# Graph propagation with hop attention: the first bucket pass carries buckets and 16-bit patterns through its products, in one stated repeated order

## The chip, the cores and the metric

The kernel runs on one core of one Trainium2 chip. The metric is the device time of one execution in microseconds (us); of several runs the median is taken, and lower is better.

## The reference, cut to what matters

A graph has N = 10000 nodes with D = 128 features, and E = 160000 edges with random sources and targets (so 16 per node). Seven times every node receives the sum of its sources' features, scaled by both degrees; then each node attends over its eight tokens, and a readout weighs the tokens into one row.

```python
h, toks = x, [x]
for _ in range(K):                       # K = 7
    msg = h[src] * deg_inv_sqrt[src, None] * deg_inv_sqrt[dst, None]
    h = _segment_sum(msg, dst, N)
    toks.append(h)
tok = jnp.stack(toks, axis=1)            # (N, 8, 128)
t = _layernorm(tok)                      # then q, k, v, softmax over the 8 tokens, wo
o = tok + ...
alpha = _softmax(_layernorm(o) @ w_r)    # readout
return jnp.einsum('nk,nkd->nd', alpha, o)
```

The edges come as two lists of 64-bit integers in no order. Most of the kernel's first tenth turns them into a form that TensorE can multiply with.

## The kernel before, in words

The kernel has four stages: the **first bucket pass** (`pass_a` and `decode`), which sorts edges by blocks of 128 target nodes; the **second bucket pass** (`place`, `matrices`), which sorts by buckets of sources and builds 0/1 matrices, together with hop 1 (`hop1`), in an order written out by hand (the table FRONT); hops 2 to 7 (`block`); and the attention (the table ORDER). The change touches the first stage and what lies directly around it.

*First bucket pass.* A partition holds 1250 edges, in 25 chunks of 50 (NCH, B). The target's block (target >> 7, one of NK = 79) is an edge's key. Ahead of the loop, integer steps on VectorE (L307 to L313) make the key and two digits of a code of 24 bits, `d1` and `d2`, source >> 3 and the rest with the target's place in its block. `lag` (L254) compares the key columns of all chunks at distance 1 to 49 on VectorE (`eq`, L264) and adds the matches up in PSUM on TensorE (L266), which numbers an edge among equal ones in its chunk and partition. `first_rows` (L187) loads the node features and scales 79 groups of 128 rows on ScalarE (L198).

Each chunk then goes through this chain. `oh` (L226, VectorE) is the one-hot of 50 keys against 79 blocks, 3950 columns. `U` (L329, TensorE, 50 matmuls with a triangular matrix) counts equal keys in the partitions above; ScalarE copies it (L337). `ux` (L239, VectorE, 3950 columns) picks each edge's own count, and `R` (L243, L244, TensorE) folds it and adds the lag's number; `rk` (L247, VectorE) is the edge's rank in its block, that is, the partition in which it is to land. One-hots of the rank are made on VectorE for the first 18 of 50 edges (`rv`, L373) and on ScalarE for 32 (`rs`, L360, one ACTIVATE for each; `rb`, L341, gives their bias). The two products `o` (L232, VectorE, six steps of 1264 or 1422 columns) multiply `oh` by the digits, and `ta` (L385, TensorE, 50 matmuls of 158 columns) moves both digits into place by the ranks. `take` (L333, VectorE) adds the two halves into `TT`.

At the third chunk, `first_table` (L200) finds the largest magnitude of the scaled features by one reduction on VectorE (L205, 10112 columns), and writes the table of hop 1 as a high and a low float16 half: the high half on ScalarE (L177), the low one on VectorE (L178), four parts each, with stores to DRAM behind them (`rows`, L180).

*Decoding.* After the last chunk, `decode` (L389) turns all of `TT` (2000 columns) into the source's bucket `kB` and a 16-bit word, by eight integer and mixed steps on VectorE (L400 to L411), and `lag_rows` (L270) compares `kB` of all chunks at distance 1 to 24 (`eq`, L281), adds them up on TensorE (L285) and copies the result to `wB` (L288). The second pass needs `kB`, `word` and `wB`; its first instruction on VectorE is the one-hot of `kB` (L226 again, 3800 columns).

*What sets the order.* In the first pass a scheduler lays the instructions out; the loop's body in the code takes one chunk's products between the next chunk's counts and ranks, and engines run their own rows in the order laid out. Pools decide how far a chunk may run ahead: `oh`, `rs`, `rk` and PSUM tiles have two buffers, `rv`, `ux` and `o` one. GpSimd has nothing to do during the loop.

Of the kernel before, what the change touches and what calls it, by code (L numbers as in the profile page):

```python
# [58 lines left out]
2S1.2 0X1 3V1 1w0.2 2g2 3d1 3K3  # L59
"""  # L60


class Hops:
# [123 lines left out]
    def first_rows(self):  # L187
        nc, A = self.nc, self.nc.scalar
        tab0 = self.tab[0]
        y = self.tab[1].bitcast(F32)  # L190
        nc.gpsimd.memset(y[:, NT - 1:, :], 0.0)
        nc.gpsimd.memset(tab0[:, NT:, :], 0.0)
        h = NT // 2
        for a, b in ((0, h), (h, NT - 1)):
            nc.scalar.dma_start(y[:, a:b, :], self.x[a * 128:b * 128, :].rearrange("(t p) d -> p t d", p=128))
        nc.scalar.dma_start(y[:N - (NT - 1) * 128, NT - 1, :], self.x[(NT - 1) * 128:, :])
        for t in range(NT):
            A.activation(y[:, t, :], y[:, t, :], AF.Copy, scale=self.disT[:, t:t + 1])  # L198

    def first_table(self):  # L200
        nc, V = self.nc, self.nc.vector
        tab0, y = self.tab[0], self.tab[1].bitcast(F32)
        with self.tc.tile_pool(name="ft", bufs=1) as sp, self.tc.tile_pool(name="ftp", bufs=1, space=PSUM) as pp:
            mc = sp.tile([128, 1], F32, name="mc")
            V.tensor_reduce(mc, y[:, :NT, :], axis=mybir.AxisListType.XY, op=ALU.max, apply_absolute_value=True)  # L205
            q = self.pow2(pp, sp, mc, 2.0 ** 40)
            V.tensor_copy(self.sinv, q[:, 1:2])
            for a in range(0, NT, 20):
                b = min(NT, a + 20)
                self.to_table(y[:, a:b, :], tab0, q[:, 0:1], a, b)  # L210
                self.rows(0, tab0, a, b, nc.sync)
            V.tensor_scalar(self.ctok[0], self.disT, self.sinv, None, op0=ALU.mult)


            m2 = sp.tile([128, 1], F32, name="m2")
            V.tensor_reduce(m2, self.dis2, axis=X, op=ALU.max)
            V.tensor_scalar(m2, m2, 64.0 * BIG, None, op0=ALU.mult)
            q = self.pow2(pp, sp, m2, 2.0 ** 8)
            V.tensor_mul(self.sinv, self.sinv, q[:, 1:2])
            V.tensor_copy(self.q2, q[:, 0:1])  # L220


    def onehot(self, pool, name, key, n, size=None, **kw):
# [3 lines left out]
                                     self.io2[:, None, :n, :].to_broadcast([128, m, n, 2]), op=ALU.is_equal)  # L227
# [5 lines left out]

    def rank(self, wp, wu, R, oh, U2, w):

        nc, T = self.nc, self.nc.tensor
        m, nk, k = oh.shape[1], oh.shape[2], 5
        ux = wu.tile([128, m, nk, 2], F16, name="ux", tag="ux")
        nc.vector.tensor_tensor(ux, oh, U2[:, None].to_broadcast([128, m, nk, 2]), op=ALU.mult)  # L239
        R = R[:, :m * k * 2].rearrange("p (j k i) -> p j k i", k=k, i=2)  # L240
        for s in range(0, nk, k):
            e = min(k, nk - s)
            T.matmul(R[:, :, :e, :], self.id16, ux[:, :, s:s + e, :], start=s == 0, stop=False, skip_group_check=True)  # L243
        T.matmul(R[:, :, 0, :], self.id16, w, start=False, stop=True, skip_group_check=True)  # L244
        rk = wp.tile([128, m, 2], F16, name="rk")
        with nc.allow_low_precision("whole numbers; those over 2048 only have to stay large"):
            nc.vector.tensor_reduce(rk, R.rearrange("p j k i -> p j i k"), axis=X, op=ALU.add)  # L247
        return rk
# [21 lines left out]
    def lag_rows(self, ep, pp, key, w, m):  # L270

        V, T, k = self.nc.vector, self.nc.tensor, key.shape[2]
        n = 512 // k * k
        W = pp.tile([128, -(-m * k // n), 512], F32, name="W")
        flat = lambda z: z.rearrange("p m k -> p (m k)")
        parts = [(b, b * n, min(m * k, b * n + n)) for b in range(W.shape[1])]
        for b, r, e in parts:
            T.matmul(W[:, b, :e - r], self.id16, self.zero16[:, :e - r], start=True, stop=False, skip_group_check=True)
        for l in range(1, m):
            eq = ep.tile(list(key.shape), F16, name="eq")  # L280
            V.tensor_tensor(eq[:, l:], key[:, l:], key[:, :m - l], op=ALU.is_equal)  # L281
            for b, r, e in parts:
                r1 = max(r, l * k)
                if r1 < e:
                    T.matmul(W[:, b, r1 - r:e - r], self.id16, flat(eq)[:, r1:e], start=False, stop=(l + 1) * k >= e,  # L285
                             skip_group_check=True)
        for b, r, e in parts:
            self.nc.scalar.copy(flat(w)[:, r:e], W[:, b, :e - r])  # L288

    def pass_a(self):  # L290
        tc, nc, V, A, T, G = self.tc, self.nc, self.nc.vector, self.nc.scalar, self.nc.tensor, self.nc.gpsimd
        with ExitStack() as c:
# [5 lines left out]
            with tc.tile_pool(name="pe", bufs=1) as ep, tc.tile_pool(name="peq", bufs=3) as eqp, \  # L298
# [5 lines left out]
                it = ep.tile([128, 3, NCOL], I32, name="it")  # L304
                V.tensor_single_scalar(it[:, 0], ed[:, 1, :, 0], 7, op=ALU.arith_shift_right)
                A.copy(key, it[:, 0])
                V.tensor_single_scalar(it[:, 1], ed[:, 0, :, 0], 3, op=ALU.arith_shift_right)  # L307
                V.tensor_scalar(it[:, 2], ed[:, 0, :, 0], 7, 7, op0=ALU.bitwise_and, op1=ALU.logical_shift_left)
                V.tensor_single_scalar(it[:, 0], ed[:, 1, :, 0], 127, op=ALU.bitwise_and)
                V.tensor_tensor(it[:, 2], it[:, 2], it[:, 0], op=ALU.bitwise_or)  # L310
# [12 lines left out]

            def count(ch):
                oh = self.onehot(wp, "oh", K4[:, ch], NK)
                U = pp.tile([128, NK], F32, name="U")
                for j in range(NP):
                    for i in range(2):
                        T.matmul(U, self.tri, oh[:, j, :, i], start=j + i == 0, stop=j + i == NP)  # L329
                return oh, U  # L330

            def take(ch, ta):
                V.tensor_reduce(self.TT[:, ch, :NK], ta.rearrange("p h k -> p k h"), axis=X, op=ALU.add)  # L333

            def ranks(ch, oh, U):
                U2 = wp.tile([128, NK, 2], F16, name="U2")
                A.activation(U2, U[:, :, None].to_broadcast([128, NK, 2]), AF.Copy)  # L337
                rk = self.rank(wp, w1, pp.tile([128, 512], F32, name="R"), oh, U2, W4[:, ch])
# [1189 lines left out]
```

## Time and profile before

| | us |
|---|---|
| median of 3 runs | 3777.88 (3774.79 to 3786.38) |
| the profiled execution | 3821.03 |
| span of its trace | 3819.1 |
| second pass's first one-hot in the trace | 378.27 |

Mean granted clock of TensorE in the span: 0.976. Busy over the span: PE (TensorE) 94%, VectorE (DVE) 79%, ScalarE (ACT) 72%, GpSimd (POOL) 44%. The span is cut into 40 slices on the page, so that a slice is 95 us and the first pass fills the first four. Its digits there are tenths of busy time: PE 5 8 8 7, DVE 8 9 9 8, ACT 6 8 8 6, POOL 0 0 0 0.

How to read the rows: in a timeline, a row has the start and the duration in us, the engine, the line of the kernel, the operation, output<-inputs, their shapes, the count of merged instructions, and in brackets the idle time before them and what ended it. In a group, the busy time and the mean in ns stand behind the first bar, idle time before them behind the second. In the view of waits: engine and line, what it waited for, us in total, times, the longest.

### The profile page before, as it was taken

How to read it: one execution, taken by the hardware profiler on the slowest of the kernel's cores; microseconds unless marked ns; L12 is line 12 of the kernel's file. 1: busy time of each engine (PE TensorE's matmuls, PEld its weight loads, DVE VectorE, ACT ScalarE, POOL GpSimd, SP SyncE). 2: the span in 40 equal slices, each digit the busy share in tenths (PEclk: the TensorE clock that was granted, in tenths of full speed). 3: DMA queues.
4: the chain of work that ended last, by engine and by line, in shares of the span. 5: the costliest groups of instructions: out<-in, count | busy, mean ns of one | idle time of the engine just before them, and what ended most of it. 6: DMA issues, size and time to landing. Idle time of an engine off the chain costs nothing.

```text
span 3819.1 us, 173439 instructions
## 1 busy us (share of the span) xinstructions
PE 3594.5 (94%) x73707; PEld 2938.2 (77%) x73707; DVE 3019.8 (79%) x6994; ACT 2767.2 (72%) x6989; POOL 1681.5 (44%) x2230
## 2 busy tenths in 40 slices
PE   5887799999899999999999999999999998999997
PEld 4665678878688888887888788788878886777775
DVE  8998888888677777777777777777766665888888
ACT  6886488888766666766676666666756668888885
POOL 0000244444356656665666566566656661121111
PEclk8998899999999999999999999999999999999998
DMA  3100356556666666666666666666666552222220
GB/s 94 49 1 1 110 184 200 193 186 194 196 198 200 201 189 205 202 198 189 201 203 202 190 201 198 191 203 201 203 186 201 187 186 78 80 77 79 82 84 15
DMA packets 332728, 595.53 MB, mean 156 GB/s; under 512 B 57448, under 2 KB 225606, under 8 KB 326694
## 3 DMA queue, kind: packets, MB, share of 16 engines
q1 hardware_dynamic: 293989, 506.70, 42.5%
q0 software_dynamic: 35392, 72.55, 6.6%
q8 instruction: 577, 9.45, 1.0%
q10 hardware_dynamic: 2560, 5.12, 0.5%
q14 instruction: 210, 1.71, 0.2%
HBM read 455.49 MB, written 128.67 MB: 153 GB/s over the span
## 4 chain that ended last, share of the span: by engine, by line
PE 78%; DVE 9%; ACT 5%; DMA 4%; issue 3%; SPq 0%; POOL 0%; POOLq 0%; ACTq 0%; DVEq 0%
PE p L801 25%; PE acc L776 24%; PE acc L761 4%; PE pv L1172 4%; PE pu L1156 3%; PE p L667 3%; ACT rs L360 2%; PE po L1191 2%; PE pt L1146 2%; DVE o L232 2%; PE acc L654 2%; ACT eb L675 2%; PE acc L655 1%; PE ur L487 1%; PE ps L1221 1%
## 5 line engine op out<-in xcount | busy, mean ns | idle before, releaser
L806 ACT ACTIVATE eb<-p 128x512 f16<-128x512 f32 x2370 | 1258.3, 602 | 510.1 <-PE p L801 290.6
L808 DVE TENSOR_TENSOR eb<-p,eight 128x512 f16<-128x512 f32 x1896 | 1220.8, 686 | 328.3 <-PE acc L776 201.8
L801 PE MATMUL p<-tab,w 128*32 128x256 f16 x34128 | 1038.3, 274 | 20.1 <-issue 13.9
L776 PE MATMUL acc<-eb,w 128*128 128x256 f16 x8532 | 1011.7, 273 | 1.2 <-issue 1.2
L801 PEld LDWEIGHTS <-w 128*32 128x32 fp8e4 x34128 | 871.6, 97 | 161.9 <-issue 142.7
L776 PEld LDWEIGHTS <-w 128*128 128x128 fp8e4 x8532 | 835.5, 98 | 99.6 <-issue 2.0
L738 POOL DMA_INDIRECT og<-tabd,oidx x541 | 561.7, 1038 | 580.4 <-PE acc L776 286.6
L738 POOL DMA_INDIRECT og<-tabh,oidx x553 | 609.5, 1102 | 361.0 <-POOL og L737 121.9
L675 ACT ACTIVATE eb<-p 128x512 f16<-128x512 f32 x695 | 378.0, 626 | 30.6 <-PE p L667 24.8
L846 POOL TENSOR_SCALAR r<-s,ctok 128x128 f32<-128x128 f32 x474 | 293.5, 619 | 43.8 <-DVE s L792 26.4
L837 ACT ACTIVATE tab<-s,c 128x128 f16<-128x128 f32 x395 | 158.5, 401 | 200.9 <-DVE eb L808 172.3
L838 DVE SCALAR_TENSOR_TENSOR tab<-s,c,tab 128x128 f16<-128x128 f32 x395 | 138.9, 352 | 180.5 <-issue 169.3
L1261 POOL TENSOR_TENSOR p<-e,in 128x1024 f32<-128x1024 f32 (+1 forms) x40 | 76.5, 1913 | 446.5 <-DVE e L1260 446.5
L1213 ACT ACTIVATE junk<-tab 128x128 f32<-128x128 f32 x626 | 248.5, 401 | 8.3 <-SPq L1497 6.7
L667 PE MATMUL p<-tab,w 128*32 128x256 f16 x5688 | 210.7, 277 | 23.3 <-issue 12.4
L360 ACT ACTIVATE rs<-iof,rb 128x128 fp8e4<-128x128 f32 x784 | 231.8, 388 | 0.3
L792 DVE TENSOR_REDUCE s<-acc 128x128 f32<-128x256 f32 x474 | 196.9, 415 | 19.4 <-PE acc L790 11.7
L654 PE MATMUL acc<-eb,w 128*128 128x129 f16 x1422 | 203.4, 223 | 1.2 <-issue 0.4
L655 PE MATMUL acc<-eb,w 128*128 128x128 f16 x1422 | 201.5, 221 | 0.1
L737 POOL COPY og<-eb 128x1 f16<-128x1 f16 x452 | 83.1, 184 | 243.5 <-ACT eb L806 243.5
L667 PEld LDWEIGHTS <-w 128*32 128x32 fp8e4 x5688 | 137.8, 97 | 63.9 <-issue 41.4
L1172 PEld LDWEIGHTS pv<-Wv,xT 128*64 128x64 f32 x2504 | 138.9, 137 | 41.2 <-ACT uT L1157 29.3
(314 smaller groups left out, 5257.6 us busy)
## 6 DMA issues: line engine op xcount, KB each, us to landing
w<-gsd SPq DMA_DIRECT2D x474, 592.0 KB
gsd<-w SPq DMA_DIRECT2D x79, 592.0 KB
tok<-r SPq DMA_DIRECT2D x546, 64.0 KB
tab<-tok SPq DMA_DIRECT2D x273, 128.0 KB
rb<-srow SPq DMA_DIRECT2D x79, 352.0 KB
tabd<-tab SPq DMA_DIRECT2D x396, 64.0 KB
ra<-srow SPq DMA_DIRECT2D x79, 224.0 KB
og<-tabh,oidx POOLq DMA_INDIRECT x553
```

Of the source, the lines that this page charges most:

```text
L360: A.activation(ro[:, j - a, i, :], self.iof, AF.Abs_reciprocal_sqrt, scale=2.0 ** 21, bias=rb[:, j - VP, i:i + 1], saturate=False)
L654: T.matmul(acc[:, :129], W, rows[:, 128:257], start=start, stop=False, skip_group_check=True)
L667: T.matmul(p[32 * w:32 * w + 32, j], q["w", g][:, NJ * 128 + s * CAP:NJ * 128 + (s + 1) * CAP], tab[:, s, :], start=True, stop=True)
L675: A.activation(e[:, :, 0:256], pv, AF.Copy, scale=8.0)
L738: self.nc.gpsimd.indirect_dma_start(out=o, out_offset=None, in_=src[0] if i == NI else src[1], in_offset=bass.IndirectOffsetOnAxis(ap=self ...
L776: T.matmul(acc[0][:, :256], w[:, J * 128:(J + 1) * 128], e[:, j, :256], start=False, stop=J == NG - 1 and not late)
L801: T.matmul(p[32 * q:32 * q + 32, j], w[:, NJ * 128 + s * CAP:NJ * 128 + (s + 1) * CAP], tab[:, s, :], start=True, stop=True)
L806: A.activation(e[:, :n, 0:256], pv, AF.Copy, scale=8.0)
L808: V.tensor_tensor(e[:, :n, 0:256], pv, self.eight[:, :, None].to_broadcast([128, n, 256]), op=ALU.mult)
L846: self.nc.gpsimd.tensor_scalar(r, s, ct[:, t:t + 1], None, op0=ALU.mult)
L1172: T.matmul(p[64 * h:64 * h + 64, u - us[0], :], S[i]["xT"][:, h * m + q, 64 * c:64 * c + 64], Wv, start=True, stop=True, tile_position=(0, ...
L1213: A.activation(j, S[i]["x"][:, g, :], AF.Square, bias=S[i]["x"][:, g, 0:1], scale=-1.0, accum_out=R[i % 6][:, 0, g:g + 1])
```

## The change

What the products carry is changed. Before, two digits; now the bucket itself (`d1` from source >> 7 and a few integer steps) and a 16-bit pattern, an integer whose bits are read as a float16 (`d2` from `w16`). So the integer steps ahead of the loop grow from five to eleven on VectorE, and after `ta` nothing is left to decode: `kw` copies both halves from PSUM into one tile KW = [kB | word] on ScalarE, `take` and `decode` go. `low` restores the part of the code that TT has to hold, by one step on ScalarE and four of 80 columns on GpSimd, per chunk. Equal buckets are counted by chunk: `eq` compares all earlier chunks with this one (chunk number × 80 columns on VectorE), `W` adds them up on TensorE (as many matmuls of 80 columns), `wB` copies on ScalarE. `eqB`, `ux` and the last two products have one buffer; `rv` and the first product now two.

`first_table` becomes a generator. Its reduction is eight reductions of ten groups; the table is written in eight parts, the high half on ScalarE, the low half by a multiplication in place and a subtraction on GpSimd (L249, L250; 1280 columns each) instead of one step on VectorE. Of the 79 scalings of feature rows, 56 stay ahead of the loop, and four more go into each of the next chunks. Constants and buffers of the second pass (`pb_constants`, memsets) are made ahead of the first pass.

The loop is written as one table, under manual order. A number ahead of a colon says by how many chunks a step is late (−1 is the next chunk); T takes the next step of `first_table` from the third turn on, Y four more scalings.

```diff
+CHUNKS = """
+-1:U 0:rs:9:12 0:rv 0:rd 0:o:0 -1:U2 1:ta -1:ux 0:rs:12:17 1:kw 1:low 0:Y 0:o:1 -1:R 0:rs:17:21 0:T 0:o:2 2:W 1:eq 0:T 0:rs:21:25 2:wB -1:rk -1:rb -2:oh
+"""
...
-            self.to_table(y[:, a:b, :], tab0, q[:, 0:1], a, b)
...
+            A.activation(tab0[:, a:b, 0:128], y[:, a:b, :], AF.Copy, scale=q[:, 0:1])
+            G.tensor_scalar(y[:, a:b, :], y[:, a:b, :], q[:, 0:1], None, op0=ALU.mult)
+            G.tensor_tensor(tab0[:, a:b, 128:256], y[:, a:b, :], tab0[:, a:b, 0:128], op=ALU.subtract)
+            yield
...
-            def take(ch, ta):
-                V.tensor_reduce(self.TT[:, ch, :NK], ta.rearrange("p h k -> p k h"), axis=X, op=ALU.add)
...
+            def kw(ch, c):
+                A.copy(self.KW[:, :, ch, :NK], c["ta"])
+
+            def low(ch, c):
+                kB, TT = self.kB[:, ch], self.TT[:, ch]
+                A.activation(TT, self.word[:, ch].bitcast(I16), AF.Copy, bias=-17407.0)
+                t = [w1.tile([128, NTP], F32, name=f"tt{i}") for i in range(2)]
+                G.tensor_scalar(t[0], kB, float(4 * NG + 1), 128.0 * (CNODES - 128), op0=ALU.max, op1=ALU.mult)
+                G.tensor_scalar(t[1], kB, 128.0 * 128, -128.0 * (CNODES - 128) * (4 * NG + 1), op0=ALU.mult, op1=ALU.add)
+                for z in t:
+                    G.tensor_tensor(TT, TT, z, op=ALU.add)
+
+            def eq(ch, c):
...
+                z = c["eq"] = w1.tile([128, last, NTP], F16, name="eqB")[:, :ch]
+                own = self.kB[:, ch, None, :].to_broadcast([128, ch, NTP])
+                V.tensor_tensor(z, self.kB[:, :ch], own, op=ALU.is_equal)
+
+            def W(ch, c):
...
+                    for k in range(ch):
+                        T.matmul(c["W"], self.id16, c["eq"][:, k], start=k == 0, stop=k == ch - 1)
...
-            self.decode()
```

On VectorE, in the middle of the loop before (one chunk; L226 is the one-hot, L232 the products, L239 ux, L247 rk, L333 the sum of the halves, L373 the one-hot of ranks):

```order
L247 TENSOR_REDUCE rk<-R 128x50 [waits PE_49]
L226 TENSOR_TENSOR oh<-key,io_228 128x3950 [waits DVE_49]
L333 TENSOR_REDUCE TT<-ta 128x79
L232 TENSOR_TENSOR o_2636<-oh,d_273 128x9x158
L232 TENSOR_TENSOR o_2636<-oh,d_274 128x9x158
L373 TENSOR_TENSOR rv<-rk,io_228 128x2304 [waits DVE_49]
L239 TENSOR_TENSOR ux<-oh,U_2641 128x3950 [waits DVE_49,Activation_49]
L232 TENSOR_TENSOR o_2637<-oh,d_273 128x8x158 [waits PE_49]
L232 TENSOR_TENSOR o_2637<-oh,d_274 128x8x158
L232 TENSOR_TENSOR o_2638<-oh,d_273 128x8x158 [waits PE_49]
L247 TENSOR_REDUCE rk<-R 128x50 [waits PE_49]
```

The same place now (the eleventh chunk's comparison; L263 is the one-hot, L269 the products, L353 ux, L366 rk, L375 the one-hot of ranks, L423 the comparison of buckets):

```order
L263 TENSOR_TENSOR oh<-key,io_228 128x3950 [waits DVE_49]
L375 TENSOR_TENSOR rv<-rk,io_228 128x2304 [waits DVE_49]
L269 TENSOR_TENSOR o_2931<-oh,d_320 128x9x158
L269 TENSOR_TENSOR o_2931<-oh,d_321 128x9x158
L353 TENSOR_TENSOR ux<-oh,U_2934 128x3950 [waits DVE_49,Activation_49]
L269 TENSOR_TENSOR o_3007<-oh,d_320 128x8x158 [waits PE_49]
L269 TENSOR_TENSOR o_3007<-oh,d_321 128x8x158
L269 TENSOR_TENSOR o_3039<-oh,d_320 128x8x158 [waits PE_49]
L269 TENSOR_TENSOR o_3039<-oh,d_321 128x8x158
L423 TENSOR_TENSOR eqB<-KW 128x800 [waits PE_49,Activation_49]
L366 TENSOR_REDUCE rk<-R 128x50
```

The sum of halves is gone, the rank's one-hot stands ahead of the first product, and the comparison, which waits for TensorE and ScalarE, stands ahead of rk and the next one-hot.

On GpSimd, what followed the memsets ahead of the pass before was the buffers of the second pass and then its gathers (L738), with nothing between:

```order
L855 MEMSET TT 128x25 [waits DVE_49,Pool_49]
L437 IOTA io_5320 128x136
L140 MEMSET eb_5329 128x520
L140 MEMSET eb_5331 128x520
L140 MEMSET eb_5333 128x520
L864 MEMSET og_5280 128x260 [waits DMAHW1_49,DVE_49,DMAHW4_49,PE_49,Activation_49]
L864 MEMSET og_5281 128x260
L864 MEMSET og_5282 128x260
L864 MEMSET og_5283 128x260
L738 DMA og_5280<-tabh_168,oidx 128x256 [waits DMAHW3_49,DVE_49,Pool_49]
```

Now GpSimd has, in the loop, `low` of every chunk (L413, L414, L416 twice) and, in four chunks, the low half of the table (tab_65 holds the scaled features, tab_64 the table):

```order
L413 TENSOR_SCALAR tt_2401<-KW 128x80 [waits Activation_49]
L414 TENSOR_SCALAR tt_2402<-KW 128x80 [waits Pool_49]
L416 TENSOR_TENSOR TT<-TT,tt_2401 128x80 [waits Activation_49,Pool_49]
L416 TENSOR_TENSOR TT<-TT,tt_2402 128x80 [waits Pool_49]
L249 TENSOR_SCALAR tab_65<-tab_65,q_2247 128x1280 [waits DMAHW0_49,DVE_49,Activation_49]
L250 TENSOR_TENSOR tab_64<-tab_65,tab_64 128x10x128 [waits Pool_49]
L249 TENSOR_SCALAR tab_65<-tab_65,q_2247 128x1280 [waits Activation_49]
L250 TENSOR_TENSOR tab_64<-tab_65,tab_64 128x10x128 [waits Pool_49]
```

All of these rows are new between the memsets and the gathers.

More of the change, by code (lines that the diff above doesn't have):

```diff
@@ L25 @@
 CELL = 334
+ROWS = 56
 CNODES = 196
@@ L232, in times @@
         self.nc.vector.tensor_tensor(out, oh, f[:, :, None, :].to_broadcast(list(oh.shape)), op=ALU.mult)
[L234 to L248, printed above, removed]
     def zeros(self, ep):
@@ L327, in count, with oh, U @@
+            C = [dict() for _ in range(NCH)]
+            def oh(ch, c):
+                c["oh"] = self.onehot(wp, "oh", K4[:, ch], NK)
+            def U(ch, c):
+                c["U"] = pp.tile([128, NK], F32, name="U")
                 for j in range(NP):
                     for i in range(2):
[L329 to L333 removed]
@@ new lines, in rk, with rb @@
+            def rk(ch, c):
+                c["rk"] = wp.tile([128, NP, 2], F16, name="rk")
+                with nc.allow_low_precision("whole numbers; those over 2048 only have to stay large"):
+                    V.tensor_reduce(c["rk"], c["R"].rearrange("p j k i -> p j i k"), axis=X, op=ALU.add)
+            def rb(ch, c):
+                c["rb"] = wp.tile([128, NP - VP, 2], F32, name="rb")
+                A.activation(c["rb"], c["rk"][:, VP:], AF.Copy, scale=-2.0 ** 21, bias=16.0)
+                c["ro"] = [None] + [wp.tile([128, b - a, 2, 128], F8, name=f"rs{a}") for a, b in cuts[1:]]
@@ new lines, in rs, with o @@
+            def rs(ch, c, a, b):
+                for j in range(a, b):
+                    k = 1 if j < VL else 2
+                    if k == 1 and ch == last:
+                        continue
+                    for i in range(2):
+                        A.activation(c["ro"][k][:, j - cuts[k][0], i, :], self.iof, AF.Abs_reciprocal_sqrt, scale=2.0 ** 21,
+                                     bias=c["rb"][:, j - VP, i:i + 1], saturate=False)
+            def o(ch, c, k):
+                a, b = cuts[k]
+                z = c["o", k] = (w1 if k else wp).tile([128, b - a, 2 * NK, 2], F16, name=f"o{a}")
+                self.times(z[:, :, :NK], c["oh"][:, a:b], D1[:, ch, a:b])
+                self.times(z[:, :, NK:], c["oh"][:, a:b], D2[:, ch, a:b])
@@ new lines, in wB @@
+            def wB(ch, c):
+                if ch:
+                    A.copy(self.wB[:, ch], c["W"])
+            F = dict(oh=oh, U=U, U2=U2, ux=ux, R=R, rk=rk, rb=rb, rv=rv, rd=rd, rs=rs, o=o, ta=ta, kw=kw, low=low, eq=eq, W=W, wB=wB)
+            sp, fp = (c.enter_context(tc.tile_pool(name=n, bufs=1, **k)) for n, k in (("ft", {}), ("ftp", dict(space=PSUM))))
+            with tc.manual_schedule():
+                more = self.first_table(sp, fp)
+                rest = list(range(ROWS, NT))
+                for it in range(-2, NCH + 4):
+                    for word in CHUNKS.split():
+                        late, z, *a = word.replace(":", " ").split()
+                        if z == "T":
+                            if it >= 2:
+                                next(more, None)
+                        elif z == "Y":
+                            if it >= 0:
+                                self.scale_rows(rest[:4])
+                                del rest[:4]
+                        elif 0 <= it - int(late) < NCH and (z != "rd" or it - int(late) == last):
+                            F[z](it - int(late), C[it - int(late)], *(int(k) for k in a))
+                for _ in more:
+                    pass
```

255 lines of the change are left out of this document (122 added, 133 removed).

## The prediction, made before the result

> **What bounds the kernel now.** I read the page first: the busy shares, then the chain that ended last.
>
> ```profile
> PE 3594.5 (94%) x73707; PEld 2938.2 (77%) x73707; DVE 3019.8 (79%) x6994; ACT 2767.2 (72%) x6989; POOL 1681.5 (44%) x2230
> PE 78%; DVE 9%; ACT 5%; DMA 4%; issue 3%; SPq 0%; POOL 0%; POOLq 0%; ACTq 0%; DVEq 0%
> ```
>
> TensorE bounds the kernel as a whole, but nearly all of that lies in the hops and the attention, which the change leaves as they are. It edits the first tenth only. What matters is when the second pass starts: everything behind it moves with it, one for one. So I went through that stretch on VectorE's timeline (start, duration), first its two ends.
>
> ```profile
> 13.46 0.80 DVE L308 TENSOR_SCALAR it<-ed 128x1250 int32<-128x1250 int32 x1
> 14.18 0.81 DVE L264 TENSOR_TENSOR eq<-key 128x1225 f16<-128x1225 f16 x1
> 14.91 1.44 DVE L310 TENSOR_TENSOR it<-it 128x1250 int32<-128x1250 int32 x1
> ...
> 40.50 0.52 DVE L264 TENSOR_TENSOR eq<-key 128x75 f16<-128x75 f16 x3
> ...
> 46.54 10.69 DVE L205 TENSOR_REDUCE mc<-tab 128x1 f32<-128x10112 f32 x1 [0.22 <-ACT tab L198]
> ...
> 65.34 1.35 DVE L373 TENSOR_TENSOR rv<-rk,io 128x2304 f16<-128x2304 f16 x1
> ```
> ```profile
> 345.26 0.32 DVE L333 TENSOR_REDUCE TT<-ta 128x79 f32<-128x158 f32 x1
> 348.25 0.32 DVE L333 TENSOR_REDUCE TT<-ta 128x79 f32<-128x158 f32 x1 [2.67 <-PE ta L385]
> ...
> 360.11 1.15 DVE L281 TENSOR_TENSOR eq<-kB 128x1920 f16<-128x1920 f16 x1
> ...
> 378.27 2.14 DVE L226 TENSOR_TENSOR oh<-kB,io 128x3800 f16<-128x3800 f16 x1 [0.28 <-PE W L285]
> ```
>
> Prologue to 65, 25 chunks to 345.26, then 33.0 us in which nothing but the decoding and the 24 row lags runs, until the second pass's first one-hot at 378.27. Next, one chunk on each engine, the group of the half copies of the table (L177), R once more where it ran slowly, and who TensorE waited for.
>
> ```profile
> 127.47 1.35 DVE L373 TENSOR_TENSOR rv<-rk,io 128x2304 f16<-128x2304 f16 x1
> 128.74 0.81 DVE L232 TENSOR_TENSOR o<-oh,d 128x1264 f16<-128x1264 f16 x1
> 129.46 2.21 DVE L239 TENSOR_TENSOR ux<-oh,U 128x3950 f16<-128x3950 f16 x1
> 131.59 2.27 DVE L232 TENSOR_TENSOR o<-oh,d 128x1264 f16<-128x1264 f16 x3
> 133.82 0.42 DVE L247 TENSOR_REDUCE rk<-R 128x50 f16<-128x250 f32 x1
> 134.16 2.21 DVE L226 TENSOR_TENSOR oh<-key,io 128x3950 f16<-128x3950 f16 x1
> 136.28 0.31 DVE L333 TENSOR_REDUCE TT<-ta 128x79 f32<-128x158 f32 x1
> 136.51 1.70 DVE L232 TENSOR_TENSOR o<-oh,d 128x1422 f16<-128x1422 f16 x2
> 138.13 1.35 DVE L373 TENSOR_TENSOR rv<-rk,io 128x2304 f16<-128x2304 f16 x1
> ```
> ```profile
> 128.60 0.21 ACT L341 ACTIVATE rb<-rk 128x32 f32<-128x32 f16 x1
> 128.72 0.27 ACT L337 ACTIVATE U<-U 128x158 f16<-128x158 f32 x1
> 128.90 9.45 ACT L360 ACTIVATE rs<-iof,rb 128x128 fp8e4<-128x128 f32 x32
> 138.26 0.21 ACT L341 ACTIVATE rb<-rk 128x32 f32<-128x32 f16 x1
> ```
> ```profile
> L177 ACT ACTIVATE tab<-tab,q 128x2560 f16<-128x2560 f32 x3 | 7.1, 2412 | 0.0
> ```
> ```profile
> 131.73 2.03 PE L243 MATMUL R<-ux,id 128*128 128x250 f16 x16 [1.36 <-DVE ux L239]
> ...
> 136.44 2.10 PE L329 MATMUL U<-oh,tri 128*128 128x79 f16 x50
> ```
> ```profile
> 205.72 3.26 PE L243 MATMUL R<-ux,id 128*128 128x250 f16 x16 [2.45 <-DVE ux L239]
> ```
> ```profile
> PE R L243 <- DVE ux L239: 20.4, 19, 2.6
> ```
>
> VectorE takes 138.13 − 127.47 = 10.66 us for a chunk and has no gap in it; ScalarE takes 138.26 − 128.60 = 9.66 and TensorE has slack (the last row, of the view of waits: it waited 20.4 us in 19 places for the product ux). So VectorE sets the pitch. From first rv to the last sum the loop has 345.26 − 65.34 = 279.9 us. Rows of one engine overlap by about 0.08, so I go by differences of starts.
>
> **The change part by part.** Prologue: the lag is now queued behind the new integer work. Against before there are three TENSOR_SCALARs more (14.18 − 13.46 = 0.72 each, 2.2) and three SCALAR_TENSOR_TENSORs (taken like L310's integer step, 1.36 each, 4.1); the last addition is another form, between 0.7 and 2.8, and I take 0.6 above the old one; eight constants moved ahead of it, about 0.1 each, 0.9. Sum 7.8, call it 8. The lag before ended at 40.9, 4.25 of it two one-hots that stood in it (2.12 each by the chunk's rows), so 36.7; after, 44.7. Then the ramp in one chain, since nothing is laid out ahead any more: one-hot 2.1, counts 3.3 (2.10 times the 1.6 by which R was slower at 205.72 behind an idle stretch), their copy 0.3, ux 2.1, ranks 3.26 + 0.2, rk 0.35, the next one-hot 2.1: 13.7. The loop starts at 58.4 instead of 65.3. The big reduction (10.69) no longer stands in the way; it comes back below.
>
> Loop: VectorE loses the sum (136.51 − 136.28 = 0.23) and gets a comparison of (chunk number) × 80 columns. The largest, 1920 columns, takes 1.07 net by the row at 360.11, the smallest like any short step about 0.1; so 0.07 + 0.042 per chunk. VectorE needs 10.43 + 0.07 + 0.042·n. In the written order a longer chain closes: the comparison of chunk n−1 has one buffer, is read by W of n−1 on TensorE, and W stands behind R, which waits for ux. rk, one-hot, rv, the first product pair and ux take 0.34 + 2.12 + 1.27 + 1.62 + 2.13 = 7.5; R 2.0 + 0.2; W at most 0.042 per chunk (U's row, 50 matmuls in 2.10); two handovers and the comparison itself. I put P(n) = 10.42 + 0.08·n. Over 24 periods: 250 + 22 = 272. ScalarE gets three short copies, 10.1 in all, and hides.
>
> The table building: eight reductions of 10.69 / 8 = 1.34 in four chunks, +11 on VectorE (before, the same 10.69 stood ahead of the loop). Scaling 23 rows on ScalarE makes the first chunks 1.2 longer for it, of which about 3 us show in all. Short steps 2.5. In chunks 8 to 11 ScalarE has two half copies (2412 / 2 = 1.2 each): 10.1 + 2.5 = 12.65 instead of 11.2, 1.5 × 4 = 6. The loop comes to 272 + 11 + 3 + 2.5 + 6 = 294.5; 58.4 + 294.5 = 353.
>
> Tail: the last chunk's rv, its second compare (between rv's 1.3 and ux's 2.1, taken at 2.1 because it writes as many columns in a narrow type), six products 4.5, then the last two comparisons with W between, 3.9: 353 + 11.8 = 365. So the serial 33.0 us shrink to 3.9, the loop grows by some 14 and the prologue gives 7 back: 378.3 − 365 = **13 us less**, if nothing else happens.
>
> GpSimd is what else. It gets work it never had beside this loop: per chunk four steps of 80 columns, and in each of chunks 8 to 11 twice a multiplication and a subtraction of 1280 columns, both from SBUF, in place of 11 us on VectorE. All long steps of VectorE in the loop have two SBUF operands. The trace has few such meetings:
>
> ```profile
> 3206.44 1.95 POOL L1261 TENSOR_TENSOR p<-e,in 128x1024 f32<-128x1024 f32 x1 [14.21 <-DVE e L1260]
> 3207.05 1.39 DVE L1304 TENSOR_TENSOR rx<-v 128x16 f32<-128x16 f32 x1
> L846 POOL TENSOR_SCALAR r<-s,ctok 128x128 f32<-128x128 f32 x474 | 293.5, 619 | 43.8 <-DVE s L792 26.4
> L838 DVE SCALAR_TENSOR_TENSOR tab<-s,c,tab x395: 341/352/355, 1061.4 to 2816.2; 128x128 f16<-128x128 f32 x198
> ```
>
> A 16-column step of VectorE, issued while GpSimd's two-operand step ran, took 1.39 us and ended at 3208.44, just behind GpSimd's end at 3208.39: it was held for the rest of it. Against that stands L838, two operands as well, beside GpSimd's one-operand L846 (619 ns): 395 times, 341 to 355 ns, never held long. So a subtraction holds VectorE, and a multiplication somewhere between nothing (L838) and its whole length. Sizes: 1.95 × 1280 / 1024 = 2.4 for the subtraction; the multiplication, by the same slope, no longer than that; I take 1.0, nearer to L838's row. Two of each per chunk hold 2 × 2.3 + 2 × 1.0 = 6.6 us. VectorE then needs 10.85 + 6.6 + 0.7 = 18.15 in those chunks where 12.65 were to be had: 5.5 × 4 = 22. The four small steps hold about 0.7 per chunk (0.15 to 0.6 for 80 columns, two with one operand), of which the wait for W hides some 0.4: 25 × 0.25 = 6. Together 28, bounds 0 and 45. Net −13 + 28 = **+15**.
>
> The Trainium skill, SBUF — State Buffer, section "Who interferes with whom", says that VectorE with two SBUF inputs and a GpSimd instruction that reads SBUF exclude each other for the whole instruction. L1304 agrees (1.39 us for 16 columns); L838's 395 rows do not. By that sentence the multiplications would hold for their full 2.4 too and the sum would be about +26.
>
> The durations are those of the profiled execution, 3821.03 us; the shown runs have a median of 3777.88, 43 less. The shift is carried over in microseconds: 3777.9 + 15 = 3793.
>
> **The rivals.** *No hold (A), the other side.* If a step of GpSimd only waits for VectorE, which is busy nearly all the time, and VectorE never for it, the 28 fall away: 3765, and 3750 if the chain through W closes sooner than I put it. For it: L838. Against: L1304. It decides from under half of the 28. *Only two-operand steps hold (C).* Then chunks 8 to 11 cost 4.9 + 0.3 on VectorE's 10.85, 3.4 × 4 = 14, the small ones vanish in the wait for W: −13 + 14, 3779, no change. *Every GpSimd step holds for its whole length (D):* 12.65 becomes 21, 34 + 6 and something for the queue behind: 3804. *TensorE loses its clock between chunks (B).*
>
> In the row at 205.72 the same 16 matmuls that took 2.03 took 3.26, behind an idle 2.45. In the new order U, the pair products and R leave a gap of about 2.4 in every chunk, ahead of R, and R is on the closing chain: 1.2 × 24 = 29 on top of the forecast, 3822. Against it: the loop had 19 such waits of up to 2.6 before, and the row at 131.73 is a fast one. In the Trainium skill, TensorE: Matmul & The Clock Gate, section "HAM oscillation — how this bites in real kernels", a gap has to be over about 3.4 us; by that B would not come, though the row at 205.72 is slow behind 2.45. *That the change does not do what it says:* the first one-hot of the second pass also waits on GpSimd; were it the last chunk's four steps, some 1.5 us more, inside every case.
>
> **How the numbers follow.** Forecast 0.37, A 0.28, C 0.13, D 0.08, B 0.09, and 0.05 for a loop that simply runs shorter than my chain. About 0.3%, 11 us, is what a measurement of this kernel tells from no change. Slower by more: 0.29 of the forecast, 0.08 of D, 0.09 of B, 0.01 of C: 0.47. Faster: 0.18 of A, 0.02 of C, the 0.05: 0.25. Within: the rest, 0.28. The range runs from A's middle less its own spread, 3758, to 3818, short of B; the forecast's own is 3783 to 3808.
>
> **What would show it.** Right: the second pass's first one-hot near 393; chunks 8 to 11 about 18 long, with oh, ux and the products there stretched beyond 2.2 and 0.8 and ending just behind a GpSimd step; the other chunks 10.6 to 12.5; under 5 us from the last product to that one-hot. Wrong in the hold: the stretched rows missing and the one-hot at 365 (A) or 379 (C). Wrong in the clock: R over 3 us in most chunks. Wrong in the chain: the comparison never waiting for W, with a pitch of 10.5 throughout. The prediction as a whole is wrong if the time falls by more than 11 us.

## The result, and the profile after

The changed kernel takes 3827.12 us (median of 4 runs, 3823.57 to 3828.5), before on the same chip 3780.65: a ratio of 1.0122, with a 95% interval of 1.0103 to 1.014. So it is 46 us slower; 15 were forecast, and the result lies 9 us above the range. The profiled execution has a span of 3826.7 us. The second pass begins at 425.30 us where it began at 378.27: 47.0 later; the medians differ by 46.5, so that this is the whole loss. The two traces can't be compared behind that point: the one of before comes from an execution of 3821.03 us and has 3440.8 there, the one after has 3401.4. That the rest is unchanged, as the prediction had it, rests on the agreement of 47.0 with 46.5.

The end of the first stage in the new trace, the last chunk's one-hot of ranks, the last two comparisons and the second pass's first one-hot:

```profile
411.08 1.36 DVE L375 TENSOR_TENSOR rv<-rk,io 128x2304 f16<-128x2304 f16 x1
...
419.51 1.10 DVE L423 TENSOR_TENSOR eqB<-KW 128x1840 f16<-128x1840 f16 x1
422.95 1.16 DVE L423 TENSOR_TENSOR eqB<-KW 128x1920 f16<-128x1920 f16 x1 [2.33 <-PE WB L429]
425.30 2.14 DVE L263 TENSOR_TENSOR oh<-KW,io 128x3800 f16<-128x3800 f16 x1 [1.19 <-PE WB L429]
```

One quiet chunk of the changed loop, VectorE's timeline (L263 one-hot, L269 products, L353 ux, L423 comparison of buckets, L366 rk, L375 one-hot of ranks):

```profile
383.88 2.20 DVE L263 TENSOR_TENSOR oh<-key,io 128x3950 f16<-128x3950 f16 x1
386.00 1.35 DVE L375 TENSOR_TENSOR rv<-rk,io 128x2304 f16<-128x2304 f16 x1
387.27 1.70 DVE L269 TENSOR_TENSOR o<-oh,d 128x1422 f16<-128x1422 f16 x2
389.32 2.22 DVE L353 TENSOR_TENSOR ux<-oh,U 128x3950 f16<-128x3950 f16 x1 [0.35 <-ACT U L349]
392.22 3.05 DVE L269 TENSOR_TENSOR o<-oh,d 128x1264 f16<-128x1264 f16 x4 [0.69 <-PE ta L403]
396.06 1.09 DVE L423 TENSOR_TENSOR eqB<-KW 128x1680 f16<-128x1680 f16 x1 [0.78 <-ACT rs L389]
397.07 0.41 DVE L366 TENSOR_REDUCE rk<-R 128x50 f16<-128x250 f32 x1
397.39 2.20 DVE L263 TENSOR_TENSOR oh<-key,io 128x3950 f16<-128x3950 f16 x1
```

TensorE in the same chunk, and what it waited for over the whole loop (the last row is of the view of waits):

```profile
386.13 2.81 PE L345 MATMUL U<-oh,tri 128*128 128x79 f16 x50 [3.69 <-DVE oh L263]
388.75 2.28 PE L403 MATMUL ta<-o,rv 128*128 128x158 f16 x18
390.87 2.46 PE L403 MATMUL ta<-o,rs 128*128 128x158 f16 x32
393.17 2.04 PE L360 MATMUL R<-ux,id 128*128 128x250 f16 x16
395.04 0.19 PE L361 MATMUL R<-wl,id 128*128 128x50 f16 x1
395.07 0.88 PE L429 MATMUL WB<-eqB,id 128*128 128x80 f16 x20
```
```profile
PE U L345 <- DVE oh L263: 102.1, 24, 8.9
```

Read as one ring: the one-hot ends at 386.08, U begins at once, the pair products, R and W follow without a gap up to 395.95, the comparison begins at 396.06, then rk, then the next one-hot. (The comparison may not overwrite its one buffer before W has read it. The view names ScalarE for its wait in this chunk, and W in five of the chunks before it, from 317.77 to 369.09.) A period of 397.39 − 383.88 = 13.5 us in which VectorE waits in three places and TensorE stands idle for 3.69, and is slow right behind it: 50 matmuls of U in 2.81 (2.10 before), 18 of the pair products in 2.28 (1.48 a chunk in the old loop). The granted clock says the same, third from the end of these rows (before it the busy times of PE, PEld, DVE, ACT and POOL), first for the four long chunks, then for quiet ones; the loop before had 0.94 between 120 and 345 us:

```profile
181.03:268.37 87.34, 45.35 (x504) 41.07 (x505) 85.94 (x51) 55.02 (x165) 80.40 (x32) 0.68 0.23 65
300.00:400.00 100.00, 71.30 (x1008) 67.61 (x1006) 89.31 (x86) 82.34 (x290) 25.82 (x32) 0.90 0.01 2
```

One of the four chunks in which GpSimd makes the table's low half, GpSimd and then VectorE:

```profile
202.46 5.56 POOL L249 TENSOR_SCALAR tab<-tab,q 128x1280 f32<-128x1280 f32 x1
208.11 3.16 POOL L250 TENSOR_TENSOR tab<-tab,tab 128x1280 f16<-128x1280 f32 x1
211.25 4.88 POOL L249 TENSOR_SCALAR tab<-tab,q 128x1280 f32<-128x1280 f32 x1
216.22 4.00 POOL L250 TENSOR_TENSOR tab<-tab,tab 128x1280 f16<-128x1280 f32 x1
220.31 0.93 POOL L413 TENSOR_SCALAR tt<-KW 128x80 f32<-128x80 f16 x1
```
```profile
202.51 2.20 DVE L263 TENSOR_TENSOR oh<-key,io 128x3950 f16<-128x3950 f16 x1
204.64 4.15 DVE L375 TENSOR_TENSOR rv<-rk,io 128x2304 f16<-128x2304 f16 x1
208.71 4.12 DVE L269 TENSOR_TENSOR o<-oh,d 128x1422 f16<-128x1422 f16 x2
212.75 5.00 DVE L353 TENSOR_TENSOR ux<-oh,U 128x3950 f16<-128x3950 f16 x1
217.67 5.66 DVE L269 TENSOR_TENSOR o<-oh,d 128x1264 f16<-128x1264 f16 x4
```

Both engines are shown busy without a gap, and both are stretched: rv takes 4.15 for 1.35, ux 5.00 for 2.21, and the multiplications and subtractions of GpSimd vary from 3.79 to 6.34 and from 2.60 to 4.01. They look as if they took turns; the experiments test it.

### The profile page after: what moved, and what is told of

Read it like the earlier page. It is cut to its first block, busy times and chain, and to the rows that moved or that the text cites. A ratio compares the mean times of both kernels' runs of the same rounds, so it can differ in the third digit from the quotient of the medians.

```text
span 3826.7 us, 174086 instructions
## 1 busy us (share of the span) xinstructions
PE 3564.1 (93%) x73922; PEld 2965.1 (77%) x73922; DVE 3046.0 (80%) x6969; ACT 2735.2 (71%) x7060; POOL 1826.3 (48%) x2348
## 4 chain that ended last, share of the span: by engine, by line
PE 80%; DVE 9%; DMA 5%; issue 3%; ACT 3%; POOL 1%; SPq 0%; ACTq 0%; DVEq 0%; POOLq 0%
PE p L843 25%; PE acc L818 24%; PE pv L1219 4%; PE acc L803 4%; PE pu L1203 4%; PE po L1238 2%; PE p L709 2%; PE pt L1193 2%; DMA ra<-srow 2%; PE ta L403 2%; DVE oh L263 2%; PE acc L696 2%; ACT eb L717 1%; PE U L345 1%; DVE o L269 1%
## 5 line engine op out<-in xcount | busy, mean ns | idle before, releaser
L848 ACT ACTIVATE eb<-p 128x512 f16<-128x512 f32 x2370 | 1212.9, 609 | 521.1 <-PE p L843 516.0
L850 DVE TENSOR_TENSOR eb<-p,eight 128x512 f16<-128x512 f32 x1896 | 1180.2, 683 | 298.6 <-PE p L843 297.1
L843 PE MATMUL p<-tab,w 128*32 128x256 f16 x34128 | 1026.2, 274 | 5.1 <-DVE same L1127 4.6
L717 ACT ACTIVATE eb<-p 128x512 f16<-128x512 f32 x695 | 374.2, 622 | 14.1 <-PE p L709 10.9
L880 DVE SCALAR_TENSOR_TENSOR tab<-s,c,tab 128x128 f16<-128x128 f32 x395 | 168.3, 426 | 180.5 <-ACT tab L879 180.5
L709 PE MATMUL p<-tab,w 128*32 128x256 f16 x5688 | 204.3, 278 | 22.5 <-ACT eb L717 14.5
L834 DVE TENSOR_REDUCE s<-acc 128x128 f32<-128x256 f32 x474 | 196.6, 415 | 15.3 <-PE acc L832 11.8
```

The costliest lines, as they stand in the source:

```text
L709: T.matmul(p[32 * w:32 * w + 32, j], q["w", g][:, NJ * 128 + s * CAP:NJ * 128 + (s + 1) * CAP], tab[:, s, :], start=True, stop=True)
L717: A.activation(e[:, :, 0:256], pv, AF.Copy, scale=8.0)
L843: T.matmul(p[32 * q:32 * q + 32, j], w[:, NJ * 128 + s * CAP:NJ * 128 + (s + 1) * CAP], tab[:, s, :], start=True, stop=True)
L848: A.activation(e[:, :n, 0:256], pv, AF.Copy, scale=8.0)
L850: V.tensor_tensor(e[:, :n, 0:256], pv, self.eight[:, :, None].to_broadcast([128, n, 256]), op=ALU.mult)
```

## The experiments

Two theories stood at first. H: GpSimd's large steps hold VectorE. O: the written order closes the ring above. The measure is the start of the second pass in each trace. The chips differ: before took 3781, 3819, 3807 and 3779 us (medians) in the result and the three groups of runs, and on the second the stretch behind the second pass took 3438 us instead of 3401; the first stage agrees (first rank one-hot at 59.5 to 60.1 wherever its order was not changed). So times are given as ratios to before on the same chip. The second pass's start is read from one trace of each kernel. Its shift against before agrees with that of the medians within about 4 us, but for two kernels: all three steps early (38 us in the trace, 46 in the medians) and the last one (−3 and −11). Why these two differ stays open.

| kernel | second pass begins, us | ratio to before, 95% interval |
|---|---|---|
| before | 378.27 | 1 |
| after | 425.30 | 1.0122, 1.0103 to 1.014 |
| low half on VectorE | 419.01 | 1.0091, 1.0066 to 1.0115 |
| W first | 435.24 | 1.0149, 1.0124 to 1.0175 |
| W first, one-hot early | 425.13 | 1.0117, 1.0093 to 1.014 |
| gap filled | 409.43 | 1.006, 1.0039 to 1.0082 |
| subtraction only | 409.32 | one run |
| multiplication only | 408.65 | one run |
| low half on VectorE, late | 405.26 | 1.0076, 1.0052 to 1.0099 |
| all three early (W, its copy, the one-hot) | 416.26 | 1.0125, 1.0109 to 1.0142 |
| all three early, low half late | 393.21 | 1.0054, 1.0034 to 1.0074 |
| one-hot early | 401.29 | 1.0059, 1.0044 to 1.0074 |
| one-hot early, low half late | 375.62 | 0.9974, 0.9961 to 0.9987 |
| no small steps | 423.52 | not comparable |

**GpSimd's large steps taken away.**

```diff
-            G.tensor_scalar(y[:, a:b, :], y[:, a:b, :], q[:, 0:1], None, op0=ALU.mult)
-            G.tensor_tensor(tab0[:, a:b, 128:256], y[:, a:b, :], tab0[:, a:b, 0:128], op=ALU.subtract)
+            V.scalar_tensor_tensor(tab0[:, a:b, 128:256], y[:, a:b, :], q[:, 0:1], tab0[:, a:b, 0:128], op0=ALU.mult, op1=ALU.subtract)
```

> The low half of the table goes back to VectorE: one step of 1280 columns in place of GpSimd's multiplication and subtraction, everything else as after the change. Theory H (GpSimd's two steps hold VectorE): the chunks 9 to 12, now 21.5, 24.2, 24.1 and 17.5 us from one rank one-hot to the next, fall to 15 or 16 although VectorE gets two steps of 1.4 more in each; the time falls by 24 to 30 us, to about 3800. Rival O (the written order alone makes the loop long, and these chunks are long because ScalarE has two more copies in them): VectorE's two steps come on top and the time stays or rises by up to 6 us. Rival C (TensorE's lowered clock in these chunks, 0.68, is a cause and not a result): under 10 us.

Only 6 us were gained, of 24 to 30 expected. The stretched rows are gone, but a new wait stands in their place. VectorE's timeline of this kernel:

```profile
201.31 1.55 DVE L249 SCALAR_TENSOR_TENSOR tab<-tab,q,tab 128x1280 f16<-128x1280 f32 x1 [3.81 <-ACT tab L248]
```

VectorE needs the high half that ScalarE makes in the same place of the table, behind 8 of its one-hots: 3.81 us in each of the four chunks. So this run could not decide; the step was then put two parts later.

```diff
+        for i in range(len(parts) + 2):
+            if i < len(parts):
+                a, b = parts[i]
+                A.activation(tab0[:, a:b, 0:128], y[:, a:b, :], AF.Copy, scale=q[:, 0:1])
+            if i >= 2:
+                a, b = parts[i - 2]
+                V.scalar_tensor_tensor(tab0[:, a:b, 128:256], y[:, a:b, :], q[:, 0:1], tab0[:, a:b, 0:128], op0=ALU.mult, op1=ALU.subtract)
```

> The low half of the table again on VectorE, now two parts behind ScalarE's high half, so that no step waits for it (where it was at once, VectorE waited 3.8 us in each of the four chunks for ScalarE, which hid what GpSimd's leaving gave). Theory H2: the chunks 8 to 12, 100.8 us after the change, fall to 70 to 76, the second pass begins 25 to 31 us earlier than 425.3, and the kernel is 15 to 22 us slower than before where the change was 46.5 slower. Rival O (these chunks are long by their order): they stay over 85, and less than 12 us are gained.

VectorE's timeline of this kernel has the same step without a wait:

```profile
192.30 1.55 DVE L253 SCALAR_TENSOR_TENSOR tab<-tab,q,tab 128x1280 f16<-128x1280 f32 x1
```

The chunks 8 to 12 (13.4, 16.3, 15.2, 16.1, 14.9 between rank one-hots) add up to 75.9 instead of 100.8, and the second pass begins 20.0 us earlier; the other 5 are lost again in other chunks, 1.3 of them in the one behind. H is right in kind; 20 is under the 25 expected.

**Which of the two large steps holds.** One is left out at a time (its line is deleted; for the second, a memset of the same columns stands in place of the subtraction; the low half is then made of unscaled rows, or is zero).

> GpSimd's multiplication is left out, the subtraction stays, so the low half of the table is computed from unscaled rows. Theory H2 (GpSimd and VectorE exclude each other for whole instructions, both kinds alike: in the four chunks 10.9 us of VectorE and 10.6 of GpSimd stand one behind the other, 21.5 in all): about half of GpSimd's time goes, the chunks 9 to 12 fall from 21.5, 24.2, 24.1, 17.5 to 15 to 17, the second pass begins 18 to 24 us earlier, near 404. Rival H1 (only the two-operand subtraction excludes, the multiplication does not): the four chunks keep nearly their length, less than 6 us earlier.

> GpSimd's multiplication stays, its subtraction is replaced by a memset of the same columns, which reads nothing, so the low half is zero. Theory H2 (the multiplication excludes VectorE for its whole length): the second pass begins 12 to 20 us earlier than 425.3, as where the subtraction alone was kept, and VectorE's long steps are stretched by the multiplication's length beside it. Rival H1 (the multiplication does not hold): 30 us or more earlier, with no step of VectorE stretched beside a multiplication.

16.0 and 16.7 us earlier: leaving out either is worth nearly the same, and both hold. (16.0 is under the 18 to 24 expected, 16.7 within the 12 to 20.) With the subtraction alone, GpSimd and VectorE:

```profile
183.51 7.11 POOL L249 TENSOR_TENSOR tab<-tab,tab 128x1280 f16<-128x1280 f32 x2 [1.29 <-ACT tab L248]
```
```profile
182.26 2.20 DVE L262 TENSOR_TENSOR oh<-key,io 128x3950 f16<-128x3950 f16 x1
184.39 3.77 DVE L374 TENSOR_TENSOR rv<-rk,io 128x2304 f16<-128x2304 f16 x1
188.07 4.12 DVE L268 TENSOR_TENSOR o<-oh,d 128x1422 f16<-128x1422 f16 x2
192.12 2.20 DVE L352 TENSOR_TENSOR ux<-oh,U 128x3950 f16<-128x3950 f16 x1
```

Two subtractions, two stretched places: 3.77 − 1.35 = 2.42 and 4.12 − 1.70 = 2.42; ux beside nothing keeps its 2.20. With the multiplication alone:

```profile
201.68 4.90 POOL L249 TENSOR_SCALAR tab<-tab,q 128x1280 f32<-128x1280 f32 x1
206.53 1.16 POOL L250 MEMSET tab<- 128x1280 f16 x1
207.68 4.56 POOL L249 TENSOR_SCALAR tab<-tab,q 128x1280 f32<-128x1280 f32 x1
```
```profile
203.87 4.33 DVE L353 TENSOR_TENSOR ux<-oh,U 128x3950 f16<-128x3950 f16 x1 [0.61 <-ACT U L349]
208.12 5.79 DVE L269 TENSOR_TENSOR o<-oh,d 128x1264 f16<-128x1264 f16 x4
```

ux is 2.1 longer than its 2.21, the four products 2.8 longer than 2.99. So a multiplication holds for 2.1 to 2.8 us, about as long as a subtraction. A chunk is then VectorE's own 11 and some 2 × 2.4 + 2 × 2.4 of GpSimd, 20.6; the four chunks after the change took 21.5, 24.2, 24.1 and 17.5, on average 21.8.

**The small steps.**

> GpSimd's four steps of 80 columns in each chunk are left out, so that TT holds a wrong code; the large steps stay. Theory H2: their 1.5 to 2.5 us per chunk exclude VectorE, but fall mostly where VectorE waits for TensorE anyway; in the four long chunks, where GpSimd and VectorE stand one behind the other, 1.5 to 3 us each: the second pass begins 5 to 12 us earlier. The prediction had 6. Rival (small steps do not hold): under 2 us.

The second pass begins 1.8 us earlier, under the 5 to 12 expected and within what the rival allowed: they cost next to nothing. In the loop as a whole nothing changes (351.1 instead of 351.4 us from the first to the last one-hot of ranks). The rest lies behind it: beside the last chunk's small steps the six products take 5.03 us, without them 4.61, and the 32 pair products that follow 3.84 and 2.76. In the quiet chunks VectorE's steps beside them are stretched by under 0.2 (a one-hot of ranks of 1.51 for 1.35), while the first small step takes 0.48 to 2.08 itself: here it is mostly GpSimd that is held. With TT wrong, later stages take a long fallback path (37250 GpSimd instructions instead of 2348, a span of 127 ms), so that nothing behind the second pass's start is used of this run.

**The order.** First W was moved, alone (the first added line) and with the one-hot (the second).

```diff
--1:U 0:rs:9:12 0:rv ... 0:o:2 2:W 1:eq 0:T 0:rs:21:25 2:wB -1:rk -1:rb -2:oh
+2:W -1:U 0:rs:9:12 0:rv ... 0:o:2 1:eq 0:T 0:rs:21:25 2:wB -1:rk -1:rb -2:oh
+2:W -1:U 0:rs:9:12 0:rv ... 0:o:2 -2:oh 1:eq 0:T 0:rs:21:25 2:wB -1:rk -1:rb
```

> Only the place of W in the table is changed: it comes ahead of U instead of behind R, so that the comparison of buckets no longer waits for it. Theory O1 (the chunk's period is closed by U, the pair products, R, W, then the comparison, rk and the next one-hot, one behind the other): W and the waits of the comparison (10.1 us in the trace) leave the chain; the products then wait for the pair products on TensorE instead, so 8 to 14 us of it are gained, to about 3815. Rival H (GpSimd alone explains the excess): less than 4 us. The prediction's own chain (through ux) would have it at about 14 us too, since W was in it.

> W ahead of U, and the next but one one-hot of keys right behind the last product, ahead of the comparison and rk. Theory O1 (U waits for the one-hot that VectorE makes last in a chunk, 102 us in the trace, and everything else of the chunk stands behind U): the period goes from 13.0 to 13.5 in the quiet chunks to 11.0 to 11.8, and the time falls by 30 to 45 us, to about 3790. The chain that the prediction used runs through ux and not through U: by it the one-hot's place would not matter and the gain is that of W alone, about 14. Rival H: less than 4 us.

Both missed: 9.9 us later, and no change. TensorE's timeline with W alone moved:

```profile
347.06 0.77 PE L429 MATMUL WB<-eqB,id 128*128 128x80 f16 x17 [3.56 <-ACT wB L433]
347.66 2.91 PE L345 MATMUL U<-oh,tri 128*128 128x79 f16 x50
```

W has one buffer in PSUM, and its copy wB stands at the end of ScalarE's chunk. So W waits for the copy of the chunk before, and U now stands behind W. That takes away what the order was to give: the loop is 1.7 us longer with W alone, 6.4 shorter with the one-hot moved too. The larger loss is at the loop's end. There W of the last chunk but one stands ahead of the last pair products, and they wait with it: from the last one-hot of ranks to the second pass it is 22.2 and 23.8 us instead of 14.2. A third try moved the copy behind U2 as well:

```diff
-2:W -1:U ... -1:U2 1:ta ... 0:rs:21:25 2:wB -1:rk -1:rb
+2:W -1:U ... -1:U2 2:wB 1:ta ... 0:rs:21:25 -1:rk -1:rb
```

> W ahead of U, its copy wB behind U2 (with W alone moved, W waited for the copy of the chunk before, which ScalarE makes at its chunk's end, and U stood behind it), and the one-hot ahead of the comparison and rk. Theory O1 (the quiet chunk is closed by one-hot, U, pair products, R, W, comparison, rk one behind the other, with TensorE idle for 3.7 us and slow behind it): quiet chunks fall from 11.6 to 13.5 to what VectorE needs, 10.9 to 11.9, with U near 2.1; the four long ones keep their length. Second pass 18 to 30 us earlier, near 400; 17 to 28 us slower than before. Rival: the pitch is set elsewhere (ScalarE, or GpSimd's small steps), less than 8 us.

> Both edits in one. If H2 and O1 hold and are two causes, their gains add up: 45 to 58 us, the second pass begins between 367 and 380, and the kernel is as fast as before within 0.3% or a little faster. If they are one cause seen twice, it stays over 15 us slower than before.

9.0 us earlier alone, 32.1 together with the late low half, well under what was expected. The second kernel stays 20 us slower than before, which its expectation had as the sign of one cause seen twice; but 9.0 and 20.0 alone make 29.0, so the gains did add up, and it is the 9.0 that is small. The wait is another one now. Of the kernel with all three early, a row of the view of waits, and the last comparison on VectorE:

```profile
PE WB L429 <- DVE eqB L423: 84.6, 23, 5.5
```
```profile
413.54 1.16 DVE L423 TENSOR_TENSOR eqB<-KW 128x1920 f16<-128x1920 f16 x1 [6.90 <-ACT KW L407]
```

The comparison that W reads stands behind the one-hot on VectorE, so W ahead of U holds U until after both. And the end is long here too, 19.3 us instead of 14.2, since the last comparison waits 6.90 us for the copy behind the late pair products; the loop itself is 12.1 shorter. W was better where it stood. The last try moves one word only:

```diff
--1:U ... 0:o:2 2:W 1:eq 0:T 0:rs:21:25 2:wB -1:rk -1:rb -2:oh
+-1:U ... 0:o:2 -2:oh 2:W 1:eq 0:T 0:rs:21:25 2:wB -1:rk -1:rb
```

> One word of the table is moved: the one-hot of the next but one chunk stands right behind the last product, ahead of the comparison and rk; W stays behind R. (Where W stood ahead of U, it waited there for the copy, then for the comparison of the chunk before, 85 us, and U behind it.) Theory O1: U now waits for nothing but the one-hot, and comparison, rk and the next chunk's first steps run on VectorE beside U and the pair products; quiet chunks fall from 11.6 to 13.5 to 10.9 to 11.9, U to about 2.1; the four long chunks stay near 21.5 to 22. The second pass begins 20 to 30 us earlier than 425.3 and the kernel is 15 to 27 us slower than before. Rival: W stands in the way here too, or the chain is another one; less than 8 us.

24.0 us earlier, as expected: quiet chunks take 11.5 to 11.9, and the four long ones stay at 21.4 to 22.0. VectorE, then TensorE:

```profile
350.33 2.22 DVE L263 TENSOR_TENSOR oh<-key,io 128x3950 f16<-128x3950 f16 x1
352.46 1.10 DVE L423 TENSOR_TENSOR eqB<-KW 128x1520 f16<-128x1520 f16 x1
353.49 0.40 DVE L366 TENSOR_REDUCE rk<-R 128x50 f16<-128x250 f32 x1
```
```profile
352.60 2.11 PE L345 MATMUL U<-oh,tri 128*128 128x79 f16 x50 [1.77 <-DVE oh L263]
...
364.54 2.72 PE L345 MATMUL U<-oh,tri 128*128 128x79 f16 x50 [2.69 <-DVE oh L263]
```

Comparison and rk run beside U now. From one one-hot to the next (350.33 to 362.23) VectorE has no wait any more, so it alone sets the pitch.

**The clock.** Needless matmuls fill the gap ahead of U, and nothing else is changed.

```diff
+                if ch:
+                    for n in range(60):
+                        T.matmul(c["U"], self.tri, C[ch - 1]["oh"][:, n % NP, :, 0], start=n == 0, stop=n == 59)
```

> 60 needless matmuls of 79 columns stand ahead of U, on the one-hot of the chunk before, so that TensorE works in the gap of 3.7 us in which it waits for the new one-hot; what they write is overwritten. Theory C (U at 2.8 to 2.95 instead of 2.1 and the pair products at 4.3 to 4.6 instead of 3.7 are slow because TensorE has just stood idle): both return to the fast figures, 1.2 to 1.5 us of each quiet chunk are gained, 20 to 30 us in all, to about 3802. Rival: the gap has no such effect, or the chain does not run through U; then nothing changes or the time grows by the needless work, 0 to 10 us.

15.9 us earlier, with 60 matmuls more in each chunk. TensorE (L345 is the needless group here, L348 U itself):

```profile
357.44 2.55 PE L345 MATMUL U<-oh,tri 128*128 128x79 f16 x60
361.19 2.10 PE L348 MATMUL U<-oh,tri 128*128 128x79 f16 x50 [1.21 <-DVE oh L263]
363.13 1.47 PE L406 MATMUL ta<-o,rv 128*128 128x158 f16 x18
```

U and the pair products are back at 2.10 and 1.47, the granted clock is 1.00 from 300 to 390 us (0.90 from 300 to 400 without the filling), and the quiet chunks take 11.4 to 12.0. So the slow clock has its own part in the ring, and it goes when the gap is filled. The gain stays under the 20 to 30 expected; in this chunk and its neighbours VectorE's waits are down to 0.2 to 0.5 us ahead of the comparison, so that VectorE nearly sets the pitch.

**Both causes removed.** The early one-hot and the late low half together:

> The one-hot moved as in the single edit, and the low half of the table on VectorE two parts late. Two separate causes (the chunk's chain and GpSimd's exclusion of VectorE): the gains of 20 and of 20 to 30 us add up, the second pass begins at 375 to 386, and the kernel is within 0.3% of before. If the chain's slack had absorbed VectorE's extra steps in the single edit, these cost up to 11 us here and it stays 8 to 15 us slower.

```profile
375.62 2.14 DVE L266 TENSOR_TENSOR oh<-KW,io 128x3800 f16<-128x3800 f16 x1 [1.19 <-PE WB L432]
```

The gains add up and a little more (24.0 and 20.0 alone, 49.7 together): with the ring open, the late low half shortens the chunks 8 to 12 by 27.6 us instead of 24.9, and the other chunks lose 1.8 instead of 5.0. The second pass begins 2.7 us earlier than before, and the kernel is faster than before by 0.26% (0.13% to 0.39%, 5 to 15 us of 3779); the trace shows 2.7 of these, and where the others come from stays open. Against the change as it was, it is the version to keep.

## Why the prediction was wrong, point by point

The direction was right, the size was a third. What held: the first stage shifts the rest one for one (47.0 in the trace, 46.5 in the medians); the loop starts at 59.7 (58.4 forecast); the serial end shrinks from 33.0 us, though to 5.8 (419.51 to 425.30 us) and not to 3.9, and the stretch from the last rank one-hot takes 14.2 where 11.8 were given: the last comparison waits 2.33 us for W, which stands behind the last pair products on TensorE.

*The step that failed first: "In the written order a longer chain closes", with P(n) = 10.42 + 0.08·n.* I let the ring run through ux and gave the one-hot no follower on TensorE. But U is the first matmul group of a turn and reads the one-hot made last in the turn before, and the comparison, rk and the one-hot stand behind W, which stands behind R, the pair products and U. It could be read from the order alone. Outside the chunks 8 to 12 the intervals add up to 250.6 us where the sum had 238.3: 12 of the 29 us that the loop is over the forecast. (The 238.3 hold some 5 of the 6 us that the forecast had for the small steps, which cost 1.8 in all, so the ring was short by more than 12.) The run with one word moved shows that this ring is the cause: outside these chunks its intervals add up to 232.0.

*The step that was mis-sized: "the multiplication somewhere between nothing (L838) and its whole length ... I take 1.0".* It holds for 2.1 to 2.8. The chunks 8 to 12 took 100.8 instead of the 84 that the forecast gives: the other 17 us. Of these, 14.7 lie in the four chunks with the large steps (87.3 for 4 × 18.15), where eight multiplications at 2.1 to 2.8 instead of 1.0 make 9 to 14; the ring takes part in the rest, since moving the one-hot shortened the five chunks by 3.4. Such a hold was rival D, at a chance of 0.08; its 21 us per chunk is near the 21.8 measured. I had given the counter-rows of L838 too much weight: they are another operation, SCALAR_TENSOR_TENSOR. They do run beside the multiplication (L846 from 1502.75 us for 0.62, L838 from 1502.96 for 0.35); why they are not held was not tried. The sentence of the Trainium skill (SBUF — State Buffer, "Who interferes with whom") had it right for these pairs: VectorE's TENSOR_TENSOR with two SBUF inputs and GpSimd steps that read SBUF take turns for whole instructions (2.4 us each here).

*Rival B* was half right, at another place: R kept its 2.04 us, but U and the first pair products behind the gap were slow. The Trainium skill, TensorE: Matmul & The Clock Gate, section "HAM oscillation — how this bites in real kernels", puts the limit at gaps of about 3.4 us. The row behind 3.69 agrees with it, but U behind 2.69 in the early one-hot's run, at 2.72 us, was slower than its 2.11 behind 1.77. The other chunks of the changed loop show no sharp limit either: U took 2.10 behind 3.32 and 2.11 behind 3.44, but 2.74 behind 3.39. That the gap slows what follows is shown by filling it; from which length on is not. The forecast looked only at the gap ahead of R and kept the clock out of the sum.

*Rivals A and C* fell with the holds.

## What to carry to other kernels

Before pricing a written order, follow every engine's first instruction of a turn to the instruction of the turn before that releases it, and add up the ring it closes: moving one word was worth 24 us here, moving the wrong one cost 10, and 8 of these 10 lay behind the loop's last ranks, so the last turn has to be followed too. Work given to an idle engine is not free when its steps hold those of the bound engine, by 2.1 to 2.8 us each here; handing eight steps of about 1.5 us from VectorE to GpSimd cost 26 us (401.29 against 375.62). And the gap that TensorE spent waiting was paid twice here, once in the wait and once in the slower matmuls behind it.

## What the runs showed of the hardware

GpSimd is stretched as well as VectorE: its multiplication of 1280 columns took 3.79 to 6.20 us in the changed loop, while VectorE lost 2.1 to 2.8 to one. A memset of 1280 columns on GpSimd took 1.16 us each of the seven times, beside VectorE's products and beside ux.
